# One add of 2048 columns for a unit's squares, 34 split pairs instead of 37, and another searched order

## The chip, the cores and the metric

The kernel runs on one core of one Trainium2 chip. The metric is the device time of one execution in microseconds (us); lower is better. The core's engines are named as in the profile: PE is the matrix engine (PEld its weight loads), DVE the vector engine, ACT the scalar engine, POOL the general engine, SP the engine whose queue issues every transfer between HBM and the on-chip memory. The core's 16 DMA engines carry the transfers.

## The reference

Two steps follow each other. The first is an attention over channels for four batches b, with N = 5056 rows and C = 256 channels. The second is a soft mixture of experts over all B·N = 20224 rows, with 8 experts of 4 slots each (32 slots) and a hidden width F of 1024.

```python
qn = q / (np.linalg.norm(q, axis=1, keepdims=True) + 1e-06)
kn = k / (np.linalg.norm(k, axis=1, keepdims=True) + 1e-06)
s = kn.transpose(0, 2, 1) @ qn / tau
a = softmax(s, -1)                       # C x C for each batch
x = (v @ a).reshape(B * N, C)
logits = x @ phi                         # 20224 x 32
slot_input = softmax(logits, 0).T @ x    # over all rows
h = np.maximum(slot_input[e] @ w1[e], 0.0)
slot_out[e] = h @ w2[e]
out = softmax(logits, 1) @ slot_out
```

## The kernel before, in words

Work is cut into units and parts. A unit u (40 of them, 10 to a batch) is 512 rows of q and k side by side, one transfer of 1 MB into a tile raw (load_qk). For each unit ACT squares all 2048 columns (square), DVE adds the squares to the first unit's of the batch (add), and PE adds the four products k-transposed times q to a PSUM bank S (score, one call for 128 rows). A score is done in one of two ways. Unsplit, PE multiplies raw in f32. Split, ACT first rounds two row tiles (a pair) to fp32r (cast, 1024 columns), DVE computes what the rounding left (low), and PE multiplies the parts in three fp32r products instead. A pair of a unit is either split or not.

A part p (20, five to a batch) is 1024 rows of v. PE transposes some of them (turn) and ACT or DVE copies the result (turned); the others come transposed from HBM (load_vt). PE forms the logits (logits) with the batch's attention folded into phi, and later gathers v with the exponentials (gather). After the last gather the slots' input is put together (last_slots, last_back). The experts then run in two rounds r of four: up (into banks H), relu into a tile hs, flip_h and back_h (a transpose through PSUM into hT), and down with the second weights w2, in two halves h of the output channels (bank O for each). The four w2 tiles of a half are named w2_k_h, and a row of PE shows them as w_k_h. When a half's O is complete, o_copy (ob), o_fold (fo) and o_back (so) make its slots' output so. out_mul multiplies it with the weights of a batch, kept in a tile lg of that batch (lg_105 to lg_108 are batches 0 to 3), and four out_evict calls, each on ACT or DVE, bring the products op into a tile o, which store writes to HBM: 20 stores of 1 MB or a little less, five to a batch. Store (b, x, c) needs half x alone for c below 2.

All of this is written as a list of plan steps (at). ORDER, a table of numbers, says which steps are run and in which order, each engine keeps its share in that order, and steps that ORDER leaves out are not done: where two ways stand in the plan (split or not, ACT or DVE, transposed on PE or loaded), ORDER chooses. HOME gives each big tile one of 22 places of 8 KB per partition, and BANK gives each PSUM tile one of 8 banks. A tile can be written once the last reader of the tile before it at that place is done, so HOME decides what each transfer waits for; SP issues transfers in ORDER's order, and a waiting one holds all behind it.

Of the kernel before, what the change touches and what calls it, by code (L numbers as in the profile page):

```python
# [24 lines left out]
MIX = (UB - 1, 3 * UB - 1)  # L25
# [25 lines left out]
}  # L51
BANK = {
# [77 lines left out]
def colnorm_attention_soft_moe(  # L130
# [33 lines left out]
    def tiles(u):  # L164
        return 3 if u - 1 in MIX else 4
# [639 lines left out]
    def at(f, *a):  # L805
        plan.append((f, a))
# [5 lines left out]
    for u in range(NU):  # L812
# [3 lines left out]
        if u % UB:  # L816
            at(add, u, 0, 2)
            at(add, u, 2, 4)
        for j in range(tiles(u)):
            at(score, u, j, 0)  # L820
# [150 lines left out]
```

## Time and profile before

| what | value |
|---|---|
| runs | 274.37, 275.03, 275.58 us; median 275.03 |
| profiled execution | 275.52 us, span 273.7 us, mean granted PE clock 0.966 |
| busy | PE 242.6 us (89%), DVE 225.7 (82%), ACT 194.3 (71%) |
| DMA | 110.11 MB, mean 402 GB/s |
| HBM | read 89.03 MB, written 20.71 MB |

The span runs from the first to the last instruction of the program; 1.8 us of the profiled execution lie around it. The page's second part cuts the span into 40 slices of 6.84 us. An engine that is busy for most of the span need not set its length: what counts is which wait ends last in a stretch.

### The profile page before, as it was taken

Reading aid. Unit: us, or ns where it says so; the run is one execution under the profiler, and the core shown is the slowest. Engines: PE = TensorE matmul, PEld = TensorE weight load, DVE = VectorE, ACT = ScalarE, POOL = GpSimd, SP = SyncE. Lnnn points to the kernel's source line nnn. Section 1 sums busy time; section 2 is a strip of 40 time slices with the busy share of each in tenths; the row PEclk is TensorE's granted clock in tenths of the full one; section 3 lists DMA queues with packets and bytes.
Section 4 is the critical chain, followed back from the end, with each engine's and each line's share of the span. In section 5 each row is a group of like instructions: output and inputs, shape, how many; then the busy total and the mean of one; then the engine's idle time right before and its main releaser. Section 6 shows DMA issues by size and latency. Waiting matters only on the chain.

```text
span 273.7 us, 5827 instructions
## 1 busy us (share of the span) xinstructions
PE 242.6 (89%) x2386; PEld 192.2 (70%) x2386; DVE 225.7 (82%) x343; ACT 194.3 (71%) x275; POOL 9.5 (3%) x12
## 2 busy tenths in 40 slices
PE   6999999999998998999999999999989787896400
PEld 5899898988896896886998888986735552352200
DVE  1399999999999999899999899998889969766200
ACT  2799987989597877999978995575715367788300
POOL 1000000200001100002000002000000000000000
PEclk9999999999999999999999999999999999979855
DMA  7999999999999999999999999999999988999996
GB/s 273 427 416 415 421 420 418 421 413 408 421 385 408 366 402 390 419 415 414 421 411 422 415 416 417 406 419 415 419 419 417 379 345 353 420 417 424 418 415 268
DMA packets 16874, 110.11 MB, mean 402 GB/s; under 512 B 2000, under 2 KB 2000, under 8 KB 5456
## 3 DMA queue, kind: packets, MB, share of 16 engines
q1 hardware_dynamic: 16848, 109.75, 98.0%
q8 instruction: 18, 0.29, 0.4%
q14 instruction: 8, 0.07, 0.1%
HBM read 89.03 MB, written 20.71 MB: 401 GB/s over the span
## 4 chain that ended last, share of the span: by engine, by line
PE 44%; DMA 21%; DVE 18%; ACT 6%; issue 4%; SPq 0%; ACTq 0%; DVEq 0%
PE S L283 27%; DMA w<-in_moe_w_dram 12%; DVE sq L263 10%; PE vTp L403 5%; ACT o L787 4%; PE L L430 4%; DMA v<-in_v_dram 4%; DVE hl L237 3%; PE G L540 3%; PE op L765 3%; DMA x<-in_vt_dram 2%; DMA raw<-in_qk_dram 2%; ACT sq L248 2%; DMA out_dram<-o 1%; PE op_None L765 1%
## 5 line engine op out<-in xcount | busy, mean ns | idle before, releaser
L263 DVE TENSOR_TENSOR sq<-sq,sq 128x1024 f32<-128x1024 f32 x70 | 83.0, 1216 | 11.7 <-ACT sq L248 10.9
L248 ACT ACTIVATE sq<-raw 128x2048 f32<-128x2048 f32 (+1 forms) x40 | 74.7, 1889 | 12.8 <-DMA raw<-in_qk_dram 5.4
L283 PE MATMUL S<-raw 128*128 128x256 f32 (+1 forms) x344 | 80.4, 384 | 1.0 <-DMA raw<-in_qk_dram 1.0
L283 PEld LDWEIGHTS S<-raw 128*128 128x128 f32 (+1 forms) x344 | 61.4, 191 | 10.0 <-DMA raw<-in_qk_dram 1.7
L283 PE MATMUL S<-hl 128*128 128x256 f32 x444 | 66.3, 296 | 0.0
L283 PEld LDWEIGHTS S<-hl 128*128 128x128 f32 x444 | 57.5, 190 | 2.2 <-issue 0.6
L237 DVE TENSOR_TENSOR hl<-raw,hl 128x1024 fp32r<-128x1024 f32 x37 | 44.1, 1212 | 0.7 <-ACT hl L232 0.7
L232 ACT CAST hl<-raw 128x1024 fp32r<-128x1024 f32 x37 | 37.6, 1045 | 4.7 <-DMA raw<-in_qk_dram 3.6
L787 ACT COPY o<-op 128x512 f32<-128x512 f32 x46 | 23.7, 615 | 7.5 <-PE op L765 5.7
L765 PE MATMUL op<-lg,so 32*128 32x512 f32 x128 | 22.9, 666 | 4.9 <-ACT o L787 2.3
L403 PE MATMUL vTp<-ident,v 128*128 128x128 f32 x168 | 23.3, 275 | 0.4 <-DMA v<-in_v_dram 0.4
L408 ACT COPY x<-vTp 128x512 f32<-128x512 f32 x35 | 19.6, 586 | 4.4 <-PE vTp L403 4.3
L403 PEld LDWEIGHTS vTp<-ident,v 128*128 128x128 f32 x168 | 19.1, 142 | 2.2 <-DMA v<-in_v_dram 0.6
L430 PE MATMUL L<-x,M 128*32 128x256 f32 (+1 forms) x320 | 19.2, 378 | 1.0 <-DMA x<-in_vt_dram 1.0
L540 PE MATMUL G<-v,dn 128*32 128x256 f32 x320 | 19.6, 381 | 0.1
L765 PEld LDWEIGHTS op<-lg,so 32*128 32x128 f32 x128 | 8.9, 193 | 14.8 <-ACT o L787 8.8
L785 DVE COPY o<-op 128x512 f32<-128x512 f32 x18 | 11.8, 682 | 9.0 <-PE op L765 6.4
L430 PEld LDWEIGHTS L<-x,M 128*32 128x32 f32 x320 | 10.4, 110 | 7.7 <-issue 1.1
L540 PEld LDWEIGHTS G<-v,dn 128*32 128x32 f32 x320 | 10.9, 110 | 5.2 <-issue 0.7
L304 POOL TENSOR_TENSOR rn<-nt,half 128x4 f32<-128x4 f32 x4 | 7.8, 1938 | 110.6 <-DVE nt L299 110.6
L449 ACT COPY lg<-L 128x256 f32<-128x256 f32 x20 | 7.0, 370 | 5.6 <-PE L L430 4.2
L722 PEld LDWEIGHTS O<-w,hT 128*32 128x32 f32 x256 | 7.0, 110 | 4.5 <-issue 2.9
(112 smaller groups left out, 213.4 us busy)
## 6 DMA issues: line engine op xcount, KB each, us to landing
raw<-in_qk_dram SPq DMA_DIRECT2D x37, 1024.0 KB, 10.3
v<-in_v_dram SPq DMA_DIRECT2D x20, 1024.0 KB, 9.8
w<-in_moe_w_dram SPq DMA_DIRECT2D x16, 1024.0 KB, 12.2
out_dram<-o SPq DMA_DIRECT2D x16, 1024.0 KB, 6.7
x<-in_vt_dram SPq DMA_DIRECT2D x15, 512.0 KB, 8.7
out_dram<-o SPq DMA_DIRECT2D x4, 960.0 KB, 9.3
raw<-in_qk_dram SPq DMA_DIRECT2D x3, 768.0 KB, 6.8
x<-in_vt_dram SPq DMA_DIRECT2D x4, 480.0 KB, 9.1
```

The lines of the kernel that those rows point to most:

```text
L232: act.copy(hl[:, :, 0::2, :], raws[u][:, 2 * k : 2 * k + 2])
L237: dve.tensor_tensor(hl[:, :, 1::2, :], raws[u][:, 2 * k : 2 * k + 2], hl[:, :, 0::2, :].bitcast(F32), op=ALU.subtract)
L248: act.activation(sq_tile(u)[:, :n], raws[u][:, :n], AF.Square)
L263: dve.tensor_tensor(a[:, lo:hi], a[:, lo:hi], s[:, lo:hi], op=ALU.add)
L283: pe.matmul(sm, w, x, start=first[bb], stop=False, skip_group_check=True)
L403: pe.transpose(tp[:, P * jj : P * jj + P], vs[p][:, 4 * h + jj, P * m : P * m + P], ident)
L408: (act.copy, dve.tensor_copy)[eng](x[:, h * UT : h * UT + UT], tps[p, h, m])
L430: pe.matmul(L[S * g : S * g + S, :n, :], M[:, m, :], x[:, :n, S * g : S * g + S], start=m == 0, stop=m == 1,)
L540: pe.matmul(gp[S * g : S * g + S, :C], dn[:, x, j, :], vt[:, j, :], start=x == 0 and j < G, stop=x == n - 1 and j >= G,)
L765: pe.matmul(ops[b, x, c, g][:, o : o + n], so[S * g : S * g + S, h], mv.rearrange("s j t -> s (j t)"), start=True, stop=True,)
L785: dve.tensor_copy(dst, src)
L787: act.copy(dst, src)
```

## The change

The plan gets one more choice for a unit other than the first of its batch and the two that are shared by two batches: a single add over all 2048 columns in place of two of 1024. ORDER, HOME and BANK are replaced. Counted from the tables, before has 72 adds, all of a half unit; the change has 28 whole ones and 16 halves. Split pairs go from 37 to 34. Of the 42 copies of a transposed part, DVE does 4 instead of 7; of the 80 evictions of the output, DVE does 33 instead of 23. Transfers are the same 117, in another order.

```diff
@@ -26,103 +26,103 @@
-    "w1_2": 16, "w1_3": 18, "w1_4": 5, "w1_5": 15, "w1_6": 10, "w1_7": 19, "w2_0_0": 20, "w2_0_1": 17, "w2_1_0": 4,
-    "w2_1_1": 0, "w2_2_0": 2, "w2_2_1": 6, "w2_3_0": 8, "w2_3_1": 9, "hs0": 11, "hT0": 14, "hs1": 18, "hT1": 1,
+    "w1_7": 20, "w2_0_0": 10, "w2_0_1": 18, "w2_1_0": 2, "w2_1_1": 14, "w2_2_0": 1, "w2_2_1": 3, "w2_3_0": 11,
+    "w2_3_1": 5, "hs0": 15, "hT0": 19, "hs1": 18, "hT1": 6, "o0_0_0": 0, "o0_0_1": 15, "o0_1_0": 12, "o0_1_1": 19,
...
@@ -816,6 +816,8 @@
         if u % UB:
             at(add, u, 0, 2)
             at(add, u, 2, 4)
+            if u not in MIX:
+                at(add, u, 0, 4)
         for j in range(tiles(u)):
             at(score, u, j, 0)
         if u in MIX:
```

What the tables do is seen best in the order of each engine. First DVE at the start of the program: adds of squares (L263) and the subtractions of split pairs (L237, hl is the pair's tile). Before:

```order
L215 COPY fold_100<-fold 128x32 x4
L263 TENSOR_TENSOR sq_123<-sq_123,sq_134 128x1024 x2
L237 TENSOR_TENSOR hl_0_150<-raw_77,hl_0_150 128x4x256
L263 TENSOR_TENSOR sq_123<-sq_123,sq_171 128x1024 x2
L237 TENSOR_TENSOR hl_0_175<-raw_79,hl_0_175 128x4x256
L263 TENSOR_TENSOR sq_123<-sq_123,sq_178 128x1024
```

With the change:

```order
L215 COPY fold_100<-fold 128x32 x4
L263 TENSOR_TENSOR sq_114<-sq_114,sq_123 128x2048
L263 TENSOR_TENSOR sq_114<-sq_114,sq_129 128x2048
L263 TENSOR_TENSOR sq_114<-sq_114,sq_138 128x2048
L237 TENSOR_TENSOR hl_0_173<-raw_79,hl_0_173 128x4x256
L263 TENSOR_TENSOR sq_114<-sq_114,sq_192 128x2048
```

Adds are whole, and the first subtraction is that of unit 3 instead of unit 2, behind three units' adds.

Second, PE where the second half of O is completed with the last two weight tiles, w_0_1 and w_1_1. Before (op_0_0 of lg_108 belongs to the third store, op_1_0 of lg_105 to the fourth, op_0_1 of lg_108 to the fifth):

```order
L765 MATMUL op_0_0_3_2519<-lg_108,so 128x512
L722 MATMUL O_2459<-w_0_1_2502,hT_2328 32x128 x2
...
L722 MATMUL O_2459<-w_1_1_2504,hT_2328 32x128 x2
L738 MATMUL fo_2566<-ob_2564,fold_100 128x128
L765 MATMUL op_1_0_0_2569<-lg_105,so 128x512
...
L765 MATMUL op_1_0_3_2572<-lg_105,so 128x512
L765 MATMUL op_0_1_0_2588<-lg_108,so 128x512
```

With the change (op_0_1 of lg_108 is now the fourth store's, op_1_0 of lg_105 the fifth's):

```order
L765 MATMUL op_0_0_3_2459<-lg_108,so 128x512
L722 MATMUL O_2431<-w_2_1_2315,hT_2349 32x128 x2
...
L722 MATMUL O_2431<-w_1_1_2347,hT_2271 32x128 x2
L765 MATMUL op_0_1_0_2516<-lg_108,so 128x512
...
L765 MATMUL op_0_1_3_2519<-lg_108,so 128x512
L738 MATMUL fo_2529<-ob_2514,fold_100 128x128
L765 MATMUL op_1_0_0_2532<-lg_105,so 128x512
```

The fourth store's products stand straight behind the last down instead of behind the fold of the second half.

Third, DVE from the copy of the first half's O on (ob, L734). L658 and L665 finish the weights of a batch, L785 evicts products for a store. Before:

```order
L655 RECIPROCAL cs_2373<-cs_2373 128x40
L734 COPY ob_2435<-O_2348 128x128
L665 STREAM_TRANSPOSE lg_105<-lg_105 128x512
L640 TENSOR_REDUCE cm_2511<-lg_106 128x40
L658 TENSOR_TENSOR lg_108<-lg_108,cs_2373 128x1280
L665 STREAM_TRANSPOSE lg_108<-lg_108 128x512 x2
```

With the change:

```order
L655 RECIPROCAL cs_2367<-cs_2367 128x40
L658 TENSOR_TENSOR lg_108<-lg_108,cs_2367 128x1280
L734 COPY ob_2389<-O_2294 128x128
L665 STREAM_TRANSPOSE lg_108<-lg_108 128x512 x2
L785 COPY o_0_1_2409<-op_0_1_3_2404 128x512
L785 COPY o_0_1_2409<-op_0_1_2_2403 128x512
L785 COPY o_0_0_2423<-op_0_0_0_2415 128x512
```

The product L658 of batch 3 stands ahead of the copy instead of behind it, and DVE takes two evictions of the first store and one of the second, which ACT did alone.

## Rows read from the trace of the kernel before

**Rows 1.** The page: GB/s in 40 slices, and the queue of all transfers.
```profile
GB/s 273 427 416 415 421 420 418 421 413 408 421 385 408 366 402 390 419 415 414 421 411 422 415 416 417 406 419 415 419 419 417 379 345 353 420 417 424 418 415 268
q1 hardware_dynamic: 16848, 109.75, 98.0%
```

**Rows 2.** Windows: stretch, length, busy of each engine, PE clock, DMA share, GB/s.
```profile
90.00:100.00 10.00, 10.00 (x67) 8.75 (x60) 9.93 (x16) 8.13 (x9) 0.00 (x0) 1.00 0.95 371
100.00:210.00 110.00, 107.58 (x1313) 85.73 (x1315) 102.54 (x191) 80.39 (x143) 4.46 (x3) 1.00 1.01 415
...
217.50:220.00 2.50, 2.10 (x40) 1.14 (x41) 2.46 (x4) 1.43 (x3) 0.00 (x0) 1.00 0.60 249
...
222.00:223.00 1.00, 0.74 (x20) 0.42 (x20) 0.78 (x2) 1.00 (x2) 0.00 (x0) 1.00 0.46 188
...
228.00:229.10 1.10, 1.10 (x11) 0.58 (x14) 1.10 (x2) 1.10 (x2) 0.00 (x0) 1.00 0.13 52
...
258.00:270.00 12.00, 0.00 (x0) 0.00 (x0) 0.00 (x0) 0.00 (x0) 0.00 (x0) 0.52 1.01 421
270.00:273.70 3.70, 0.00 (x0) 0.00 (x0) 0.00 (x0) 0.00 (x0) 0.00 (x0) 0.50 0.32 135
```

**Rows 3.** Chain that ended last, 198 to 236 us: start, length, what.
```profile
201.23 21.45 DMA w<-in_moe_w_dram
...
222.72 1.97 PE O L722 x60
...
225.90 1.20 PE op L765 x8
```

**Rows 4.** Timeline, 205 to 224 us: start, length, instruction, idle time before it.
```profile
209.55 1.06 PE L722 MATMUL O<-w,hT 128*32 128x128 f32 x32
...
210.54 1.16 PE L704 MATMUL hTp<-ident,hs 128*128 128x128 f32 x8
...
215.72 1.14 PE L765 MATMUL op<-lg,so 32*128 32x512 f32 x8 [0.35 <-ACT so L744]
...
216.88 2.05 ACT L787 COPY o<-op 128x512 f32<-128x512 f32 x4 [1.21 <-PE op L765]
...
218.96 3.61 SPq L793 DMA_DIRECT2D out_dram<-o  x2
...
222.22 1.29 DVE L785 COPY o<-op 128x512 f32<-128x512 f32 x2 [1.31 <-PE op L765]
```

**Rows 5.** Stores (L793) between 226 and 240 us.
```profile
L793 SPq DMA_DIRECT2D out_dram<-o x5: 332/332/332, 228.4 to 236.5; - x5
...
DMA to landing us min/median/max: 4.1/5.9/7.2
```

**Rows 6.** Groups by shape: line, engine, operation, xcount | busy us, mean ns | idle before.
```profile
L263 DVE TENSOR_TENSOR sq<-sq,sq 128x1024 f32<-128x1024 f32 x70 | 83.0, 1216 | 11.7 <-ACT sq L248 10.9
L283 PEld LDWEIGHTS S<-hl 128*128 128x128 f32 x444 | 57.5, 190 | 2.2 <-issue 0.6 <-DVE hl L237 0.2
L237 DVE TENSOR_TENSOR hl<-raw,hl 128x1024 fp32r<-128x1024 f32 x37 | 44.1, 1212 | 0.7 <-ACT hl L232 0.7
L785 DVE COPY o<-op 128x512 f32<-128x512 f32 x18 | 11.8, 682 | 9.0 <-PE op L765 6.4 <-PE op_None L765 2.6
L288 DVE TENSOR_TENSOR sq<-sq 128x1024 f32<-128x1024 f32 x4 | 4.9, 1225 | 0.1
L408 DVE COPY x<-vTp 128x512 f32<-128x512 f32 x7 | 4.6, 676 | 0.0
L288 DVE TENSOR_TENSOR sq<-sq 128x512 f32<-128x512 f32 x4 | 2.7, 683 | 0.0
```

**Rows 7.** Chain over the whole span: an unsplit tile (x4), a split one (x6), adds.
```profile
99.19 1.14 DVE sq L263
...
112.70 0.86 PE S L283 x4
...
151.93 0.72 PE S L283 x6
```

180 rows, old and new, of tables (BANK, HOME, ORDER) are left out of this document.

## The prediction

> **What bounds the kernel now.** I read the page's slices first. The DMA queue holds the 16 engines for 98.0% of the span, and most of the 40 slices stand at 415 to 422 GB/s [rows 1]. So the transfers are the bound, and the question is where they stop. At the rate of the last full stretch, 421 GB/s [rows 2], the queue's 109.75 MB [rows 1] take 109.75 / 0.421 = 260.7 us. The span is 273.7, so 13.0 us are lost somewhere, and the windows of the thin slices say where (length × (1 − rate/421)):
>
> - the first slice, 273 GB/s over 6.84 us [rows 1]: 2.4 us, the start;
> - 90 to 100 us at 371: 1.2 us;
> - 217.5 to 220 at 249: 1.0; 222 to 223 at 188: 0.55; 228 to 229.1 at 52: 0.96;
> - 270 to 273.7 at 135: 2.5, the end [rows 2].
>
> That is 8.6; of the rest, 110 us at 415 make 1.6, and some 2.8 us are spread over thin spots that I can't name. Two of these are the subject: the loads' thin spot at 90 to 100, and the holes between loads and stores at 217 to 229.
>
> PE is the second bound: busy for 107.58 of 110 us between 100 and 210 [rows 2]. While the transfers flow this doesn't show; it decides when the first stores can leave.
>
> Next the chain that ended last, around the turn from loads to stores. The last weight tile, issued at 201.23, lands 21.45 us later, at 222.68; PE multiplies with it (1.97 from 222.72), and the products of the fourth store begin at 225.90 (1.20) [rows 3]. Between the end of the one (224.69) and the start of the other lie 1.21 us: the copy, fold and copy back of the second half of O. The fourth store is issued at 228.4 [rows 5], and the hole at 228 to 229.1 stands in front of its transfers. After it the rate is 421 until 270 with every engine idle [rows 2]. So the end is the fourth store's issue plus the bytes of what follows; whatever moves that issue moves the end, and work elsewhere moves it only through the landing of the last weight tile.
>
> **The change part by part.** *Whole adds.* An add of 1024 columns takes 1216 ns [rows 6]. No add of 2048 is in the trace. Bounds: two forms of one operation on line 288 take 683 ns for 512 columns and 1225 for 1024 [rows 6], a slope of 1.06 ns a column, so 1225 + 1024 × 1.06 = 2309 ns; from above, no saving at all, 2 × 1216 = 2432. In the chain an add that follows another counts 1.14 [rows 7], since instructions overlap; against 2 × 1.14 the saving is near nothing. I take half of the 123 ns: 28 × 0.06 = 1.7 us of DVE, with 0 and 28 × 0.123 = 3.4 as ends. *Split pairs.* Three fewer: DVE −3 × 1212 ns = −3.6 us (low) [rows 6], ACT the same number of casts less. PE does six tiles unsplit at 0.86 instead of 0.72 [rows 7]: 6 × 0.14 = +0.84 us. *Copies and evictions.* Three turned copies leave DVE (−3 × 676 ns = −2.0), ten evictions come to it (10 × 682 = +6.8) [rows 6]. DVE's sum is −1.7 − 3.6 − 2.0 + 6.8 = −0.5 us (−2.2 to +1.2), ACT is eased. All of this is hidden by the transfers, where DVE and ACT have slack against PE and PE against the queue: worth 0, with the exception of PE's +0.84, which shifts the first half's tail, and of the late place where ten evictions land. Bytes don't change.
>
> *The tail.* I follow the order from PE's first products to the fourth store. First store: products at 215.72 (1.14) [rows 4], now about 0.9 later for PE's extra work; but ACT's four evictions of 2.05 in a row [rows 4] become two on each engine, two on DVE being 1.29 [rows 4], so −0.76. The store leaves at about 219.1, as before (218.96 [rows 4]): the hole of 217.5 to 220 stays. Second store: one of its evictions goes to DVE; it leaves about 220.5 instead of 222.22 [rows 4], and may fill the hole at 222 to 223. But these bytes would only be done earlier before the same wait. Fourth store: its products need the first half alone and stand straight behind the last down, not behind the fold. 222.68 (landing) + 2.0 (down) + 1.2 (products) [rows 3] + 1.5 (two evictions on each engine behind the last product, 1.29 [rows 4], and the issue) = 227.4, against 228.4: **−1.0 us**. What is late next is the fifth store, which now has the fold in front of it: its products begin at about 224.7 + 1.2 + 1.21 = 227.1, it leaves near 229.3, while the fourth's 2.5 us of transfers (1.05 MB at 421) last from about 228.1 to 230.6. Covered. Without that cover, were the fold longer by over a microsecond, the hole would move there and the gain with it.
>
> *The loads.* The searched order charges for operands that come just in time. The only waits of PE on a subtraction are 0.2 us of 2.2 [rows 6]; PE hardly waits for DVE now. What it can mend is the thin stretch of 90 to 100 us, at most 1.2 us; but new places make new waits on the queue, and each load held holds all behind it. Bounds: −1.2 (all comes back) to +1.2 (one such thin spot more). I take **−0.5**, as the adds that free the places of raw need no low in front of them any more.
>
> *The wait that is added.* w2_0_1 goes from place 17 to place 18, which hs1 holds until round 1's transpose has read it. That transpose follows 32 calls of down (209.55) and takes 1.16 from 210.54: it ends at 211.70 [rows 4], +0.9 = 212.6. Behind that load the queue holds w2_1_1 and then the stores. The transfers of the loads ahead last until 222.68 − 2 × 2.5 = 217.7. A transfer of 1 MB lands no sooner than 4.1 us after its issue [rows 5], so the wait decides once t + 4.1 + 2.5 > 222.68, t > 216.1: 3.5 us of room. Price 0, and one for one beyond.
>
> **Sum:** −1.0 − 0.5 = −1.5 us, which makes the profiled 275.52 into 274.0. The profiled execution lies 0.5 above the median of 275.03; against that, 273.5 us.
>
> **The rivals.** *Nothing comes back* (274.3 to 275.7). The holes are shares: at 217.5 to 220 the DMA share is 0.60, at 222 to 223 it is 0.46 [rows 2], so some of the 16 engines work on while the rest have run dry. If the laggards set the landing of the last weight tile and later the end, a store that leaves 1.0 earlier only lengthens the idle time of the others. For it: 98.0% busy over the span. Against it: at 228 to 229.1 the share is 0.13 [rows 2], so there nearly all stand still. The change could also add a thin spot among the loads as large as the one that it removes, +1.2 − 1.0.
>
> *More comes back.* If the stretch of 90 to 100 and the hole of 217.5 to 220 close as well: −1.2 − 1.0 − 0.55 − 0.96 = −3.7, 271.3. Against it: the first store leaves no earlier.
>
> *Slower: long adds in front of subtractions.* DVE runs in order; a subtraction behind a 2.3 us add waits up to 1.1 us longer than behind one of 1.2, and PE's split products wait for it. At most 28 × 1.1 = 31 us if each add were hit. For it: before 210 PE has 2% of slack only [rows 2], so what it loses it does not regain. Against: PE waits 0.2 us for subtractions in the whole run [rows 6], and DVE has 7.5 us of slack in that stretch (102.54 of 110). It decides through the wait on w2_0_1: PE has to be 3.5 us late to matter and, against the −1.5, 6.4 us late (t = 219.0) for the end to be 0.5% above before. At 8 us late, a quarter of the 31: 273.5 + 220.6 − 216.1 = 278.0. A rule of the Trainium skill points this way (page "Perfetto Trace Analysis", section "Optimizing Scalar/DVE Operations"): grouping into larger operations helps an engine that is saturated, but where it is not and causes bubbles on others, "breaking up instructions may allow work to be completed sooner". By that rule the pieces of before would be right; the trace bears it out only in part, as DVE is at 93% there and PE's bubbles behind it are 0.2 us. The same section puts the fixed cost of a DVE instruction on SBUF at some 60 ns; by it 28 adds would save an estimated 1.7 us, inside my ends.
>
> **How the numbers follow.** About 0.5%, 1.4 us, is what a measurement of this kernel can tell from no change: faster is below 273.65, slower above 276.4. My forecast (the fourth store's 1.0 with up to 1.2 of the loads, or the loads giving nothing; 272.4 to 274.3) gets 0.55, of which 0.42 lie below 273.65 and 0.13 above. Nothing comes back: 0.27, all within. More comes back: 0.06. Long adds: 0.12. So faster 0.48, same 0.40, slower 0.12. The range must leave out no more than 2 in 10: from 271.2 (just under the better case) to 275.8 (the end of nothing comes back); what is left out is the slower case and a little of the edges.
>
> **What would show it.** Right: the last weight tile lands at 222 to 223; the fourth store is issued near 227.4 and the window before its transfers shows no 52 GB/s; stores three, four and five follow without a gap; an add of 2048 columns takes 2.3 us; w2_0_1 is issued near 212 to 213 and still lands before it is wanted; DVE's busy time is within 3 us of 225.7. Wrong: a slice of the loads below 370 GB/s that was not there; PE's idle time behind hl grown from 0.2 to several us; w2_0_1 issued past 216.1; the fifth store late, with the hole in front of it; or the fourth store at 227.4 and the end unmoved, which is the rival of the uneven engines.

## The result, and the profile after

The changed kernel takes 270.91 us (median of 270.77 to 270.96), the kernel before 275.30 in the same runs (274.37 to 275.93): a ratio of 0.984 (95% interval 0.981 to 0.987), 4.4 us faster. The forecast was 273.5, with a range of 271.2 to 275.8. The direction was right; the gain is three times the forecast and lies just outside the range, beyond the rival that I gave 0.06.

The profiled execution took 270.94 us, its span is 269.2. First the page's rates, queue and chain, as in [rows 1].

```profile
GB/s 279 424 416 421 418 415 416 422 415 419 413 419 414 424 413 420 416 411 421 409 419 416 416 422 410 418 414 418 418 418 419 382 402 424 417 425 424 424 423 251
...
q1 hardware_dynamic: 16848, 109.75, 99.0%
...
PE 85%; DMA 4%; ACT 3%; issue 1%; DVE 1%; DVEq 0%
```

The thin slices 366 and 345 of before are gone; 382 at the turn from loads to stores is the lowest between the first and the last. The chain that ended last (the work followed back from the last instruction, at each step to what released it) now runs through PE for 85% of the span. Before, the same line of the page was another:

```profile
PE 44%; DMA 21%; DVE 18%; ACT 6%; issue 4%; SPq 0%; ACTq 0%; DVEq 0%
```

The windows of [rows 2], and two wider ones (stretch, length, busy of PE, PEld, DVE, ACT and POOL, clock, DMA share, GB/s):

```profile
40.00:90.00 50.00, 50.00 (x339) 45.08 (x341) 48.82 (x44) 42.41 (x40) 4.46 (x2) 1.00 1.02 417
90.00:100.00 10.00, 10.00 (x107) 8.01 (x100) 9.79 (x17) 8.96 (x13) 0.93 (x2) 1.00 1.02 416
100.00:210.00 110.00, 109.36 (x1349) 87.44 (x1351) 102.43 (x181) 78.96 (x141) 2.02 (x2) 1.00 1.01 416
210.00:217.50 7.50, 6.96 (x147) 4.79 (x140) 6.44 (x10) 4.54 (x8) 0.00 (x0) 1.00 0.96 380
217.50:220.00 2.50, 2.50 (x72) 1.86 (x70) 2.36 (x5) 2.05 (x4) 0.00 (x0) 1.00 1.02 423
222.00:223.00 1.00, 0.58 (x6) 0.31 (x8) 1.00 (x2) 1.00 (x3) 0.00 (x0) 1.00 1.07 451
228.00:229.10 1.10, 0.52 (x4) 0.31 (x8) 1.10 (x2) 1.10 (x4) 0.00 (x0) 1.00 1.04 432
...
210.00:230.00 20.00, 17.12 (x291) 10.26 (x286) 16.98 (x27) 13.61 (x27) 0.00 (x0) 1.00 0.99 404
230.00:258.00 28.00, 17.02 (x112) 8.52 (x104) 17.56 (x29) 12.64 (x25) 0.00 (x0) 0.78 1.01 424
```

And those windows of the kernel before that did not stand in [rows 2]:

```profile
40.00:90.00 50.00, 49.12 (x370) 43.33 (x372) 48.81 (x54) 40.23 (x39) 3.81 (x2) 1.00 1.01 411
...
210.00:230.00 20.00, 16.63 (x307) 10.09 (x297) 16.70 (x23) 11.84 (x21) 0.00 (x0) 1.00 0.88 361
230.00:258.00 28.00, 21.36 (x150) 10.80 (x150) 18.62 (x30) 21.94 (x44) 0.00 (x0) 0.94 1.01 417
```

With the prediction's arithmetic, length × (difference of rates) / 421, the 4.5 us of span come from: the loads up to 210 us, 0.7 (40 to 90) + 1.1 (90 to 100) + 0.3 = 2.0 before rounding; the turn, 210 to 230, 2.0; the stores behind it, 0.5. I had put 0.5 on the loads, 1.0 on the turn and nothing on what follows.

The same by events. The last two weight tiles (L677) and the first six stores (L793):

```profile
L677 SPq DMA_DIRECT2D w<-in_moe_w_dram x2: 328/380/433, 209.3 to 209.7; - x2
...
DMA to landing us min/median/max: 6.9/8.0/9.0
```

The last tile is issued at 209.7 and lands 9.0 later, at 218.7; before it was 222.68 [rows 3]. From the queue's timeline, the first store (its row merges six), the third and the fourth (start, length):

```profile
215.84 10.81 SPq L793 DMA_DIRECT2D out_dram<-o  x6
...
219.84 0.33 SPq L793 DMA_DIRECT2D out_dram<-o  x1
...
223.15 0.33 SPq L793 DMA_DIRECT2D out_dram<-o  x1
```

The first store leaves at 215.84 instead of 218.96 [rows 4], the fourth at 223.15 instead of 228.4 [rows 5]. PE's products for the first store begin at 213.23 instead of 215.72 [rows 4], and its waits up to there are few (the timeline's row, then who waited for whom: us, times, longest):

```profile
213.23 2.00 PE L765 MATMUL op<-lg,so 32*128 32x512 f32 x16
```

```profile
PE gt L561 <- DVE gs L555: 0.6, 1, 0.6
PE fo L738 <- DVE ob L734: 0.4, 1, 0.4
```

Before, it waited in the same stretch (from 6 us to the first products) for loads and for DVE, 4.9 us in all instead of 1.0:

```profile
PE L L430 <- DMA x<-in_vt_dram: 1.0, 2, 0.7
PE S L283 <- DMA raw<-in_qk_dram: 1.0, 1, 1.0
PE nn L294 <- DVE sq L288: 0.9, 1, 0.9
...
PE vTp L403 <- DMA v<-in_v_dram: 0.4, 1, 0.4
PE H L688 <- DVE slT L635: 0.4, 1, 0.4
PE slp L588 <- DVE gts L566: 0.4, 1, 0.4
```

Last, the group of whole adds. One takes 2286 ns (the lower estimate was 2309):

```profile
L263 DVE TENSOR_TENSOR sq<-sq,sq 128x2048 f32<-128x2048 f32 x28 | 63.7, 2286 | 10.0 <-ACT sq L248 9.2
```

### The profile page after: what moved, and what is told of

It reads as the page before. It is cut to its first block, busy times and chain, and to the rows that moved or that the text cites. A ratio compares the mean times of both kernels' runs of the same rounds, so it can differ in the third digit from the quotient of the medians.

```text
span 269.2 us, 5767 instructions
## 1 busy us (share of the span) xinstructions
PE 242.4 (90%) x2374; PEld 193.7 (72%) x2374; DVE 225.3 (84%) x319; ACT 188.3 (70%) x265; POOL 8.6 (3%) x12
## 4 chain that ended last, share of the span: by engine, by line
PE 85%; DMA 4%; ACT 3%; issue 1%; DVE 1%; DVEq 0%
PE S L283 48%; PE vTp L403 7%; PE G L540 7%; PE L L430 7%; PE op L765 4%; DMA out_dram<-o 4%; ACT o L787 3%; PE O L722 3%; PE H L688 3%; PE wake6b L800 1%; PE op_None L765 1%; PE hTp L704 1%; PE aTp L363 1%; DVE o L785 0%; PE Mp L375 0%
## 5 line engine op out<-in xcount | busy, mean ns | idle before, releaser
L263 DVE TENSOR_TENSOR sq<-sq,sq 128x2048 f32<-128x2048 f32 (+1 forms) x42 | 80.4, 1929 | 10.1 <-ACT sq L248 9.2
L283 PE MATMUL S<-raw 128*128 128x256 f32 (+1 forms) x368 | 87.3, 386 | 0.1
L283 PEld LDWEIGHTS S<-raw 128*128 128x128 f32 (+1 forms) x368 | 66.1, 193 | 9.3 <-issue 1.3
L283 PE MATMUL S<-hl 128*128 128x256 f32 x408 | 62.2, 298 | 0.0
L283 PEld LDWEIGHTS S<-hl 128*128 128x128 f32 x408 | 53.5, 190 | 2.4 <-issue 0.9
L237 DVE TENSOR_TENSOR hl<-raw,hl 128x1024 fp32r<-128x1024 f32 x34 | 40.4, 1213 | 0.0
L232 ACT CAST hl<-raw 128x1024 fp32r<-128x1024 f32 x34 | 34.8, 1044 | 6.0 <-DVE sq L263 3.6
L787 ACT COPY o<-op 128x512 f32<-128x512 f32 x40 | 20.9, 603 | 10.5 <-PE op L765 8.1
L403 PE MATMUL vTp<-ident,v 128*128 128x128 f32 x168 | 22.7, 274 | 0.0
L785 DVE COPY o<-op 128x512 f32<-128x512 f32 x24 | 15.3, 681 | 6.9 <-PE op L765 4.8
L403 PEld LDWEIGHTS vTp<-ident,v 128*128 128x128 f32 x168 | 19.1, 141 | 1.3 <-issue 0.6
L430 PE MATMUL L<-x,M 128*32 128x256 f32 (+1 forms) x320 | 19.3, 377 | 0.1
L430 PEld LDWEIGHTS L<-x,M 128*32 128x32 f32 x320 | 11.1, 110 | 5.8 <-ACT lg L449 0.5
L503 ACT ACTIVATE el<-lg,mxs 128x256 f32<-128x256 f32 (+2 forms) x11 | 7.5, 678 | 2.1 <-DVE mxs L487 2.0
```

Source lines behind the costliest of these rows:

```text
L232: act.copy(hl[:, :, 0::2, :], raws[u][:, 2 * k : 2 * k + 2])
L237: dve.tensor_tensor(hl[:, :, 1::2, :], raws[u][:, 2 * k : 2 * k + 2], hl[:, :, 0::2, :].bitcast(F32), op=ALU.subtract)
L263: dve.tensor_tensor(a[:, lo:hi], a[:, lo:hi], s[:, lo:hi], op=ALU.add)
L283: pe.matmul(sm, w, x, start=first[bb], stop=False, skip_group_check=True)
L403: pe.transpose(tp[:, P * jj : P * jj + P], vs[p][:, 4 * h + jj, P * m : P * m + P], ident)
L430: pe.matmul(L[S * g : S * g + S, :n, :], M[:, m, :], x[:, :n, S * g : S * g + S], start=m == 0, stop=m == 1,)
```

## The experiments

Each was timed against the kernel before, whose medians in these rounds were 274.9 to 275.3. Orders are shown as plan steps instead of ORDER's numbers.

### Do the whole adds make the gain?

The changed kernel, each whole add in two pieces:

```diff
-            dve.tensor_tensor(a[:, lo:hi], a[:, lo:hi], s[:, lo:hi], op=ALU.add)
+            for i in range(lo, hi, 2):
+                dve.tensor_tensor(a[:, i : i + 2], a[:, i : i + 2], s[:, i : i + 2], op=ALU.add)
```

> The changed kernel with each of its 28 whole adds done as two adds of 1024 columns at the same place. If the new order makes the gain (operands that are there early, so that PE and the queue lose less), DVE gets 28 x 0.05 to 0.12 = 1.3 to 3.4 us more work and hides most of it: 270.6 to 271.6 us. If the whole adds themselves make the gain, at least half of the 4.4 us is lost again: 273 us or more.

270.79 us: nothing lost. The reverse, the kernel before with whole adds:

```diff
-add u 0 2; add u 2 4
+add u 0 4
 (u = 1, 2, 3, 6 to 8, 12 to 19, 21, 24, 26, 28, 31, 34 to 36, 39)
```

> The kernel before, in its own order, with one add of 2048 columns for the 23 units whose two halves stand next to each other on DVE or with other adds alone between. If the order makes the gain: 274.5 to 276, no change beyond the spread of the kernel before. If whole adds make it: 23/28 of it, 272 or less.

274.67 us, ratio 0.998 (0.997 to 1.000): 0.3 us by the medians and 0.9 at most by the interval, where 23/28 of the gain would be 3.6. The edit that names the change carries next to none of it.

### Is it PE's work?

Less PE work late: half of the experts' first product left out, in the kernel before and in the changed one.

```diff
-        for d in range(2):
+        for d in range(1):
...
-                    stop=d == 1,
+                    stop=d == 0,
```

> The kernel before, which leaves out half of the experts' first product (the second half of the channels): PE has some 3.5 us less to do between 201 and 209 us, after the last load is issued. If the landing of the last weight tile holds the fourth store and with it the end, the first three stores leave up to 3 us earlier, the hole in front of the fourth store's transfers grows by as much, and the time stays at 274.5 to 275.5. If PE's lateness at the first store sets the end, the holes of 217 to 223 us close for good: 272 to 273.5.

274.86 us, no change. The first store left at 218.04, the fourth at 226.87, behind a last tile that landed at 200.98 + 20.14 = 221.1:

```profile
200.98 20.14 DMA w<-in_moe_w_dram
```

> The changed kernel, which leaves out half of the experts' first product (as in the run on the kernel before): PE has 3.5 us less to do after 198 us. If PE alone holds the changed kernel's end: 268 or less. If the last weight tile (218.7 us) arrives together with PE, the first store may leave earlier and close what is left of the hole at 216 us (0.7 us lost between 210 and 217.5), but the fourth store still waits for the tile: 270.0 to 270.9.

270.71 us: 0.2 gained, though its first store left at 214.97, 0.9 earlier than in the changed kernel. So PE alone does not hold the changed kernel either. Now more work, the first product of experts 0 to 3 done twice in the changed kernel:

```diff
-        for d in range(2):
+        for d in (0, 1) * (2 - r):
```

> The changed kernel with the first product of experts 0 to 3 computed twice (the second time over the first): PE is some 3.6 us later from 204 us on, no load is moved but the one that waits for round 1's transpose. If in the changed kernel PE and the last weight tile arrive together, both matter: first store near 219.4 instead of 215.8, the holes are back, 272.5 to 274. If only the loads set the end there, since stores have a lead of 4 us: 270.9 to 271.5.

274.33 us: 3.4 lost for 3.4 of work (the busy time of L688 went from 7.3 to 10.7), above the range of either case. Then in the middle of the program, six transposes of v twice, in both kernels, and in the changed one with w2_0_1 freed of its wait:

```diff
-        for jj in range(4):
+        for jj in (0, 1, 2, 3) * (2 if p in (4, 5, 7) else 1):
...
-    "w2_0_1": 18,
+    "w2_0_1": 8,
```

> The changed kernel with six of its transposes of v (parts 4, 5 and 7, between 88 and 120 us) done twice, the second over the first: PE has 2.8 us more to do at a place where, by its busy share, the transfers are the bound. If PE has no slack from there to the first store (0.6 us idle before it), it is 2.8 us later there and the end follows one for one, as it did for the 3.6 us put in at 204 us: 273.0 to 274.0. If the work is hidden behind the transfers, as the prediction had it for PE's 0.84 us: 270.8 to 271.5.

> The changed kernel with the six transposes done twice, as before, and with w2_0_1 in another place, free since 190 us, so that it no longer waits for round 1's transpose. If the 2.7 us that the extra work cost went through that wait (it was issued at 211.8 instead of 209.3, and the last tile landed at 220.5 instead of 218.7): 271.5 to 272.3. If PE's first store alone carries it: 273.3 to 273.8, as with the wait.

273.65 us without the second edit, 273.78 with it: PE work of 2.8 us by estimate (the busy time of L403 grew by 2.6) cost 2.7 to 2.9. The wait on w2_0_1 isn't the way: freed of it, the last tile is issued at 204.9 and has landed by 218.6 as in the changed kernel, but the first store leaves at 218.42 and the window of 210 to 230 stands at 366 GB/s instead of 404. The store in the queue's timeline, then the window:

```profile
218.42 0.35 SPq L793 DMA_DIRECT2D out_dram<-o  x1
```

```profile
210.00:230.00 20.00, 18.14 (x338) 11.77 (x326) 15.97 (x26) 12.89 (x25) 0.00 (x0) 1.00 0.90 366
```

In the kernel before:

> The kernel before with the six transposes of v (parts 4, 5 and 7) done twice: PE has the same 2.8 us more to do as in the run on the changed kernel, here between 90 and 111 us. If PE set the pace of the kernel before too, so that what it waited less in the change (4 us up to the first store) is paid back one for one: 277.3 to 278.3. If only the transfers set it there: 275 to 275.8.

276.21 us: 1.2 of the 2.8, ratio 1.0044 (1.0028 to 1.0061), between the two cases. And less work at that place, in both kernels, leaving out half of the products of six unsplit tiles:

```diff
-        for m in range(2):
+        for m in range(1 if not split and u in (23, 25, 26) else 2):
```

> The kernel before, which leaves out half of the products of six unsplit tiles (units 23, 25 and 26): PE has 2.6 us less to do between 75 and 106 us. If PE alone set the pace: 272.3 to 273. If it waits for loads and for DVE there, part of the 2.6 us turns into waiting: 273 to 274.5. If the transfers alone set it: 274.8 to 275.4.

> The changed kernel, which leaves out the same half products: PE has 2.6 us less to do there. If PE alone holds the changed kernel: 268.5. If loads, PE and the last weight tile arrive together, as the run without half of the experts' product says: 270.2 to 270.8.

274.94 and 270.77 us: nothing in either. In the kernel before, part of the work left out became waiting, 5.9 us up to the first products instead of 4.9; of PE's waits the largest grew (L431 is L430 of the kernel before):

```profile
PE L L431 <- DMA x<-in_vt_dram: 2.0, 2, 1.7
```

So a faster PE alone would not have made the kernel before faster: it waited for loads and for DVE. In the changed kernel PE and the transfers arrive together: PE has no slack, and being earlier alone is worth next to nothing.

### What is a hole among the loads worth?

The kernel before, four loads reordered so that the add on which part 0 waits no longer holds the queue:

```diff
 load_vt 7 0
-load_v 0; load_v 4; ... load_qk 31; load_qk 32
+load_qk 31; load_v 4; load_v 0; ... load_qk 32
```

> The kernel before with four loads in another order: behind the half tile of part 7 now comes unit 31 (which waits for nothing there), then part 4, part 0 and unit 32, so that the add on which part 0 waits no longer holds the queue. The thin spot of 90 to 100 us (371 GB/s) should close. If a thin spot among the loads is paid at the end: 1.2 us by its size, and up to 1 more by what PE then waits less: 272.8 to 274.2. If it only idles engines that are ahead of the others: 274.6 to 275.6.

273.91 us, ratio 0.995 (0.993 to 0.997): 1.4 us gained, with the thin spot closed (before it stood at 371) and the waits on L430 gone:

```profile
90.00:100.00 10.00, 10.00 (x61) 8.92 (x58) 9.91 (x15) 8.09 (x9) 0.00 (x0) 1.00 1.00 412
```

The changed kernel with a hole put in:

```diff
 load_qk 32
+load_qk 33
 load_qk 39; load_v 5
-load_qk 33
```

> The changed kernel with one load moved forward in the queue: unit 33, which has to wait until 102.5 us for a place, now stands ahead of unit 39 and part 5, so that the queue runs dry for some 2.5 to 3 us near 104 us. If the landing of the last weight tile carries every hole among the loads to the end: 273.2 to 274.2. If the stores' lead or PE hides it: 270.9 to 272.

273.02 us: 2.1 lost. The window shows the hole, (1 − 262/419) × 6 = 2.2 us of transfers against the changed kernel's 419 there; the last tile (second fence, its line) landed at 210.7 + 10.5 = 221.2 instead of 218.7.

```profile
100.00:106.00 6.00, 6.00 (x84) 4.20 (x83) 5.97 (x9) 5.14 (x7) 0.00 (x0) 1.00 0.71 262
```

```profile
L677 SPq DMA_DIRECT2D w<-in_moe_w_dram x2: 327/506/684, 210.3 to 210.7; - x2
...
DMA to landing us min/median/max: 8.3/9.4/10.5
```

Better loads and less PE work together, in the kernel before:

> The kernel before with the four loads in the better order and with half of the first product left out: both earlier runs of it in one. If loads and PE hold each other in turn, the two together give more than their sum of 1.5 us: 272 to 273. If the landing of the last weight tile alone sets the end of that kernel: as the reordered loads alone, 273.5 to 274.2.

273.72 us: as the loads alone, so less PE work adds nothing there either.

### The turn to the stores

The changed kernel with its fourth and fifth store in the order of before:

```diff
-o_copy 1; out_mul 3 0 1; ... o_fold 1; o_back 1; out_mul 0 1 0; ... store 3 0 1; ... store 0 1 0
+o_copy 1; o_fold 1; o_back 1; out_mul 0 1 0; ... store 0 1 0; out_mul 3 0 1; ... store 3 0 1
```

> The changed kernel with the fourth and fifth store in the order of before: the fold and copy back of the second half, then the products of lg_105, then those of lg_108. If the place of the products behind the last down is worth the 1.0 us of the prediction: 271.7 to 272.2. If the lead of the stores (the fourth is issued 4.0 us before the third has landed) covers it: 270.7 to 271.2.

271.74 us: 0.8 lost, near the 1.0 of the prediction's term. The other way round, the kernel before with the products of lg_108 straight behind the last down:

```diff
-o_copy 1; o_fold 1; o_back 1; out_mul 0 1 0; ... store 0 1 0; ... out_mul 3 0 1; ... store 3 0 1
+o_copy 1; out_mul 3 0 1; ... o_fold 1; o_back 1; out_mul 0 1 0; ... store 3 0 1; ... store 0 1 0
```

> The kernel before with the products of lg_108's fourth store straight behind the last down, and the fold beside them, as in the change. By the prediction's term the fourth store leaves 1.0 us earlier and the end follows: 273.7 to 274.5. If holes of this kind give nothing back because some of the 16 engines are behind anyway: 274.7 to 275.7.

276.09 us, ratio 1.0034 (1.0012 to 1.0055): not faster but 0.8 slower. The hole only moved. The window of 210 to 230 went from 361 to 391, the one behind it from 417 to 396, and both together stand at 394 as before:

```profile
210.00:230.00 20.00, 16.94 (x281) 9.66 (x279) 15.87 (x22) 11.74 (x22) 0.00 (x0) 1.00 0.95 391
230.00:258.00 28.00, 21.97 (x147) 11.97 (x147) 18.41 (x29) 20.78 (x42) 0.00 (x0) 0.82 0.96 396
```

The last weight tile landed 1.6 us earlier in this execution than in the one of the kernel before, so the stores are compared by their distance from that landing (here 201.31 + 19.79 = 221.10). The fourth store left 5.3 us behind it instead of 5.75 (228.43 − 222.68), the seventh 13.9 instead of 12.6. So the edit gave 0.4 us at the fourth store and not 1.0, and took 1.3 at the seventh. First the landing and the two stores of this run, then the seventh store of the kernel before:

```profile
201.31 19.79 DMA w<-in_moe_w_dram
...
226.43 0.33 SPq L794 DMA_DIRECT2D out_dram<-o  x1
...
235.03 0.33 SPq L794 DMA_DIRECT2D out_dram<-o  x1
```

```profile
235.28 0.33 SPq L793 DMA_DIRECT2D out_dram<-o  x1
```

This execution took 274.89 us, the least of the run's twelve, so it shows the kind of the loss and not its size.

An attempt to go below the changed kernel, ACT's exponential of batch 2 moved out of the first evictions' way:

```diff
-c_exp 2
 out_mul 0 0 1
-out_evict 3 (DVE); 1 (ACT); 2 (DVE); 0 (ACT)
+out_evict 2 (DVE); 0 (ACT); 3 (DVE); 1 (ACT)
 ... store 3 0 0's last eviction
+c_exp 2
```

> The changed kernel with ACT's exponential of batch 2 (1.27 us) moved from in front of the first store's evictions to behind those of the third store, and with the four evictions of the first store in the order in which PE finishes the products. The first two stores should leave 0.4 to 0.7 us earlier. If the hole at 216 us is paid at the end: 270.2 to 270.6. If the transfers of the laggard engines cover it: 270.7 to 271.0; if batch 2's weights come late: above 271.

270.88 us, no change; in its profile the first store left at 216.1, so it wasn't earlier at all.

Last, the engines of the evictions. The changed kernel with the choice of before (23 on DVE), and the kernel before, loads reordered, with the choice of the change (33):

```diff
 store 0 0 1 of the changed kernel, and so for each store
-out_evict 3 (DVE); 1 (ACT); 2 (DVE); 0 (ACT)
+out_evict 3 (ACT); 1 (ACT); 2 (ACT); 0 (ACT)
```

> The changed kernel with the choice of engine for each eviction that the kernel before made (23 on DVE). If DVE's evictions are what lets the first stores leave early enough: the first store 0.6 to 0.8 us later, the sixth to eighth without lead, 272 to 273. If the stores' lead of 4 to 5 us covers it: 270.8 to 271.3.

> The kernel before with the four loads in the better order and with the changed kernel's choice of engine for each eviction (33 on DVE instead of 23; among the first five stores ACT does 15 instead of 17, in another mix). If the stores after the turn are late because ACT has too many evictions, the step of 1.2 to 2 us at the sixth to eighth store goes: 272 to 273. If the end only follows the last weight tile: 273.5 to 274.2, as with the loads alone; if DVE, which stands in another order there, is now late: above 274.2.

275.01 us: the whole gain is gone, more than I expected. Loads and last tile are those of the changed kernel (209.7 + 9.0 = 218.7); the stores are late. The third leaves at 223.88 instead of 219.84, and the windows fall from 404 and 424 to 354 and 375 (the line of the last tiles, the queue's timeline, the windows):

```profile
L677 SPq DMA_DIRECT2D w<-in_moe_w_dram x2: 327/548/770, 209.3 to 209.7; - x2
...
DMA to landing us min/median/max: 6.9/7.9/9.0
```

```profile
223.88 0.33 SPq L793 DMA_DIRECT2D out_dram<-o  x1
```

```profile
210.00:230.00 20.00, 16.14 (x282) 9.44 (x270) 12.45 (x20) 12.15 (x24) 0.00 (x0) 1.00 0.88 354
230.00:258.00 28.00, 21.82 (x121) 10.42 (x120) 14.96 (x23) 18.10 (x36) 0.00 (x0) 0.70 0.91 375
```

The other one: 282.15 us, 8.2 slower than with its own choice. A choice of engines from one order in the other order loses both ways, so neither run prices the ten evictions by themselves. What they show is that the end follows the stores' issues as much as the loads: with the same loads, 4.1 us hang on which engine evicts what, in the order in which the other work of DVE and ACT stands.

## Why the prediction was wrong, point by point

- **What bounds it.** Transfers, 98.0% before and 99.0% now: right. That whatever moves the fourth store moves the end: too narrow. The end follows any hole behind it too (down_first), and any before it among the loads (hole, v0_later).
- **Step that failed first: "The loads ... I take −0.5", with −1.2 as the end of the range.** I priced the one thin spot that I could name and left 2.8 us "that I can't name" in place. Measured: 2.0 us by rates up to 210, and closing that one spot alone gave 1.4. Which of the new places and orders closed the others (0.7 of it between 40 and 90) is not shown. Transfers do wait longer in the queue in the changed kernel, by the median from issue to landing:

```profile
raw<-in_qk_dram SPq DMA_DIRECT2D x37, 1024.0 KB, 11.3
v<-in_v_dram SPq DMA_DIRECT2D x20, 1024.0 KB, 11.4
out_dram<-o SPq DMA_DIRECT2D x16, 1024.0 KB, 9.4
```

and of the kernel before:

```profile
raw<-in_qk_dram SPq DMA_DIRECT2D x37, 1024.0 KB, 10.3
v<-in_v_dram SPq DMA_DIRECT2D x20, 1024.0 KB, 9.8
out_dram<-o SPq DMA_DIRECT2D x16, 1024.0 KB, 6.7
```

  But this lead does not go with the gain. In the run hole the loads wait longer still, and 2.1 us are lost; in v0_later the loads of 1 MB wait no longer than before, and 1.4 are gained. The loads of v, in hole and then in v0_later:

```profile
v<-in_v_dram SPq DMA_DIRECT2D x20, 1024.0 KB, 12.1
```

```profile
v<-in_v_dram SPq DMA_DIRECT2D x20, 1024.0 KB, 9.4
```

- **Step that failed second: "The store leaves at about 219.1, as before".** I counted PE's 0.84 us of added work and not what PE would wait less, as I had taken one group's 0.2 us [rows 6] for all that PE waits. Its waits up to the first products fell by some 4 us (lists above, 4.9 to 1.0), the products began 2.5 earlier and the hole at 217.5 to 220 closed. Of the 2.5, 1.0 may be the one execution of the kernel before: in down_first, the same kernel up to there, they began at 214.77. I had written that PE does not regain what it loses, and used it for the slower rival alone; it speaks for this direction too.
- **"Worth 0", PE's added work.** Wrong: in the changed kernel added PE work costs about one for one (pe_early, up_twice), in the kernel before 1.2 of 2.8. Less of it gives nothing in either. By that the three pairs fewer should cost up to 0.8 us rather than bring anything; the runs did not test them alone.
- **The fourth store, −1.0.** Mechanism and size right within the changed order (0.8). It left 5.3 us earlier, not 1.0, since 4.0 of it came with the last tile; the other 1.3 is the term. Taken alone, in the order of before, it is a loss: the step "the fourth's transfers last ... Covered" looked one store ahead, and the seventh was late.
- **"Until 270 with every engine idle", nothing to gain behind the fourth store.** Misread: [rows 2] show it of 258 to 270 alone, and between 230 and 258 ACT was busy for 21.94 us and DVE for 18.62. The rate there rose from 417 to 424, and the choice of engines for the evictions decides 4 us there and at the turn.
- **Whole adds.** Worth nothing, as costed; DVE's busy time went from 225.7 to 225.3 (−0.5 forecast). The slower rival fell: no subtraction stands among PE's waits above. The Trainium skill ("Perfetto Trace Analysis", "Optimizing Scalar/DVE Operations") has grouping help an engine that is saturated, and breaking up help where it is not and causes bubbles on others. Neither effect shows here: 270.79 us broken up and 270.91 grouped, with DVE at 93% between 100 and 210 us.
- **The wait on w2_0_1.** Issued at 209.3, not 212.6, and without a cost that shows: with PE late (pe_early), freeing the load of it gained nothing.
- **Nothing comes back** fell. **More comes back** (271.3) was nearest, for its reason and one more: the loads' share was larger than the stretch of 90 to 100.

What stays open: of the 4.0 us by which the last tile landed earlier, 1.6 may be that one execution of the kernel before, since the edits up_half and down_first lie behind the loads and their last tile landed at 221.1. The loads' gain is less open to this: between 40 and 210 us the rate is 411 GB/s in that execution, 412 in up_half and in down_first, and 416 in the changed kernel, 1.6 to 2.0 us. How the gain divides can't be read off: the last two runs show that order and eviction engines only work together, and no run tests the new places, the three split pairs or the copies by themselves.

## What to carry to other kernels

Where transfers and an engine both stand near 98%, price waits in both directions. In this case PE's waiting for late operands was time that a better order could give back; work added to PE cost about all of itself in the changed kernel and about half in the kernel before, and taking work away brought next to nothing in either. When one late step is mended, look for the next late one several steps on, not one. And compare two executions from an event that both share, such as the landing of the last load: here it moved by 1.6 us between executions with the same loads.

## What was not expected of the hardware

The scatter differs from kernel to kernel. The changed kernel's four runs lie within 0.2 us (270.77 to 270.96), and the four with broken adds within 0.2 (270.72 to 270.88); those of the kernel before, same bytes and same instructions to within a few per cent, spread over 2.2 us (274.05 to 276.24 in one set of 25). The kernel before with a hole closed still spread over 2.6 (272.75 to 275.39), the changed one with a hole put in over 0.6 (272.67 to 273.27). What sets it is not shown: with more PE work and the order of loads unchanged, the changed kernel spread over 1.1 us in up_twice (274.12 to 275.20) and over 3.1 in pe_early (273.47 to 276.54), twelve runs each.
